# A gated mix of attention and a spectral filter on one core: input and inverse transform folded on GpSimd, one pool of exponential buffers, two chunks normalised by block transposes

## Chip, core and metric

The kernel runs on one core of one Trainium2 chip. The metric is the device time of one execution in microseconds (us); lower is better. A core has a matrix engine (TensorE, PE in the profile, with its weight loads listed apart as PEld), a vector engine (VectorE, DVE), an activation engine (ScalarE, ACT), a general-purpose engine (GpSimd, POOL) and an engine that only issues transfers here (SyncE, SP). SBUF is the working memory on the core, PSUM the accumulator memory to which TensorE writes.

## What is computed

Attention over 16 heads of 28 columns, and a two-dimensional real Fourier filter, both on the same x, mixed row by row by a sigmoid gate:

```python
def reference(A_x, A_wqkv, A_wo, B_x, B_w_r, B_w_i, gate_w):
    # x is [1, 2048, 448] bfloat16; H = 16 heads, Dh = 28
    def _A_ref(x, wqkv, wo):
        qkv = (x @ wqkv).reshape(B, S, 3, H, Dh).transpose(2, 0, 3, 1, 4)
        q, k, v = qkv[0], qkv[1], qkv[2]
        p = softmax(einsum("bhqd,bhkd->bhqk", q, k) * Dh ** -0.5)
        o = einsum("bhqk,bhkd->bhqd", p, v)
        return o.transpose(0, 2, 1, 3).reshape(B, S, D) @ wo
    def _B_ref(x, w_r, w_i):
        X = rfft2(x.astype(float32), axes=(-2, -1)) * (w_r + 1j * w_i)
        return irfft2(X, s=(S, D), axes=(-2, -1)).astype(bfloat16)
    x = A_x
    g = sigmoid((x * gate_w).sum(-1, keepdims=True))
    return g * _A_ref(x, A_wqkv, A_wo) + (1 - g) * _B_ref(x, B_w_r, B_w_i)
```

The filter takes A_x as its input too (B_x is not used). With 448 columns there are F = 225 frequencies along a row, and 2F = 450 real numbers per row after that transform.

## The kernel before

**Attention.** The heads form four groups of four (g), the 2048 queries four blocks of 512 (qc). A *chunk* is one group with one block: chunk c = 4g + qc, 16 chunks in order. A chunk has 64 *units*, one for each of 16 key tiles (kt) and four heads (j); a unit is a 128 x 512 tile of scores. TensorE makes the scores in PSUM (L1059). Most units get their exponential on ScalarE, two units to an instruction of 128 x 1024 (L1082, from the two `psA` tiles). The others, called D units here, are done on VectorE by an integer trick: `z` turns a 128 x 512 score tile in a `psX` bank into the bit pattern of a bfloat16 power (L1113), and two *shifts* add constants to it (L1137, on a pair of units, 128 x 1024 int16), so that three terms together approximate the exponential. The second shift is always on GpSimd, the first goes to VectorE or GpSimd. An A unit is one value product on TensorE (L1154), a D unit three. Value products accumulate in one bank, `psV`, for the chunk; one row of it holds the sum of the exponentials.

**Normalisation.** When a chunk's products are complete, `close` copies `psV` to `Oraw` (DVE), sends the sums through DRAM and back (`dS`, `Ssm`), inverts them and multiplies by the gate's odds (L1208, L1209, DVE), sends the result through DRAM into a broadcast tile `Rbc`, and multiplies on GpSimd into the block's `qT` tile (L1215), which is free by then. The last chunk instead goes through `finale`: 32 x 32 block transposes on DVE from `psV` and back (L1239 to L1248), in two halves, with no transfer.

**Filter.** Beside the attention run *fillers*: projections, and the transform in stages. `fa`: x times cosines and sines along the columns, four products over 112 rows each of the transposed x (`xT`) with 450 columns moving; `fae`: eviction to `bufB` (L689); `fb`: a 128-point transform over the rows with the constant `C1`, 450 columns; `fbe`: eviction (L694); `fx`: a transfer that rearranges `bufB` into `bufA`. Then per group of frequencies `fc`, the filter products `fm` (DVE, L718), `fy`/`fz` (GpSimd, L724, L726), `fd`, and `fde` (eviction to `VT`). `fp`: the inverse along the columns, four products of 448 moving columns for each of 16 tiles; `fpe`: eviction to `bufB` (L752). `output`: the last row transform (`C1T` times `bufB`) and the four groups' output projection accumulate in one bank, `oe` scales it into `fin` (L787 on DVE, L789 on ACT), `od` sends it out. Output tiles 4qc to 4qc+3 need the four normalised chunks of block qc, so tiles 8 to 11 wait for chunk 14, tiles 12 to 15 for chunk 15.

**Order.** Nothing is scheduled on the chip. While the program is built, a planner (`plan`, `dispatch`, `pick`) plays the five engines with assumed durations and writes each engine's instructions out in the order in which it started them; each engine then runs its list in that order and waits for its operands. `scores` issues a group of two A units and at most one D unit; `want_D` decides on the D unit from the VectorE and GpSimd work that the planner has outstanding, and needs a free pool entry. Exponentials of A units go to nine buffers `PA`, those of D units to four buffers `PZ` of three pairs each; at the start, until the values of the first group exist, the `PZ` buffers are lent to the A units (`early`), and no unit is a D unit in that time. Three `psX` banks serve all fillers and the D units.

## Time and profile before

| | |
|---|---|
| median of the runs | 408.09 us (410.72, 402.36, 408.09) |
| the profiled execution | 403.12 us, its span 401.3 us |
| mean granted TensorE clock in it | 0.995 |
| transfers | 18.40 MB on the queue that SP issues to, 22.6% of the 16 DMA engines' time |

The span runs from the first to the last instruction of the profiled execution; the time holds a little more than the span (1.8 us here). Busy times of an engine count overlapping instructions once. Groups of instructions are listed as line, engine, operation, what it writes and reads, shapes, count | busy time, mean duration of one | idle time of the engine ahead of them and what ended it.

### The profile page before, as it was taken

The page shows a single profiled execution, that of the slowest core. Times are in us where ns is not written, and L with a number is a line of the kernel's source. Part 1 is how long each engine was busy: PE and PEld are TensorE (multiplying, and loading weights), DVE is VectorE, ACT ScalarE, POOL GpSimd, SP SyncE. Part 2 cuts the span into 40 slices and gives each one's busy share as a digit, 9 for nine tenths or more (in the row PEclk, how much of TensorE's full clock was granted, in tenths as well). Part 3 has the DMA queues.
Part 4 walks back from the last instruction along what each step waited for, and adds up shares of the span by engine and source line. Part 5 has one row for each costly group of instructions (what it writes and reads, how often), then busy time and mean ns, then how long its engine had stood idle before and what let it go on. Part 6 is the DMA issues. An engine that isn't in the chain of part 4 may idle for free.

```text
span 401.3 us, 12448 instructions
## 1 busy us (share of the span) xinstructions
PE 378.2 (94%) x5140; PEld 127.5 (32%) x5140; DVE 328.2 (82%) x584; ACT 374.8 (93%) x415; POOL 239.0 (60%) x242
## 2 busy tenths in 40 slices
PE   6999999999998999998999999999999998999974
PEld 6553323323222222222333333333222222223232
DVE  0456697887999899998989999999989998888732
ACT  3999999999998999999999999999999999999932
POOL 4203355365566675745979899977739577654410
PEclk9999999999999999999999999999999999999989
DMA  7700014001974611114232211211010101010102
GB/s 212 184 5 2 4 6 69 3 4 32 93 98 67 69 27 35 32 26 99 82 67 56 65 47 42 73 26 42 4 28 3 29 5 29 15 59 20 54 9 93
DMA packets 41932, 19.19 MB, mean 48 GB/s; under 512 B 27884, under 2 KB 39524, under 8 KB 41876
## 3 DMA queue, kind: packets, MB, share of 16 engines
q1 hardware_dynamic: 41876, 18.40, 22.6%
q8 instruction: 40, 0.66, 0.7%
q14 instruction: 16, 0.13, 0.1%
HBM read 14.40 MB, written 2.09 MB: 41 GB/s over the span
## 4 chain that ended last, share of the span: by engine, by line
PE 41%; ACT 31%; DVE 13%; issue 8%; POOL 3%; DMA 2%; SPq 1%; DVEq 0%; ACTq 0%; POOLq 0%
ACT PA L1082 29%; PE psX L324 14%; PE psA L1059 13%; PE psV L1154 10%; DVE PZ L1113 6%; DVE PZ L1137 1%; POOL PZ L1137 1%; ACT PZ L1082 1%; PE psA L324 1%; DMA Wst<-in_B_w_r_dram 1%; PE psX L375 1%; DVE Rsm L1209 1%; PE psX L421 1%; DVE bufB L689 1%; DVE fin L787 1%
## 5 line engine op out<-in xcount | busy, mean ns | idle before, releaser
L1082 ACT ACTIVATE PA<-psA 128x1024 bf16<-128x1024 f32 x383 | 354.1, 1098 | 4.6 <-PE psX L1059 2.4
L1137 POOL TENSOR_SCALAR PZ<-PZ 128x1024 int16<-128x1024 int16 (+1 forms) x152 | 164.1, 1080 | 93.6 <-DVE PZ L1113 76.4
L1113 DVE TENSOR_SCALAR PZ<-psX 128x512 int16<-128x512 f32 x236 | 157.8, 682 | 21.8 <-PE psX L1059 19.2
L1059 PE MATMUL psA<-qT,kT 32*128 32x512 bf16 x788 | 152.5, 383 | 7.7 <-ACT PA L1082 7.1
L1154 PE MATMUL psV<-PZ,V 128*32 128x512 bf16 x730 | 117.9, 383 | 2.4 <-DVE PZ L1137 1.4
L1154 PE MATMUL psV<-PA,V 128*32 128x512 bf16 x766 | 115.5, 386 | 0.5 <-ACT PA L1082 0.5
L1059 PE MATMUL psX<-qT,kT 32*128 32x512 bf16 x236 | 90.5, 384 | 0.1
L1059 PEld LDWEIGHTS <-kT 32*128 32x128 bf16 x1024 | 42.3, 90 | 145.6 <-issue 143.5
L1137 DVE TENSOR_SCALAR PZ<-PZ 128x1024 int16<-128x1024 int16 (+1 forms) x90 | 54.8, 610 | 1.3
L1154 PEld LDWEIGHTS <-V 128*32 128x32 bf16 x1496 | 32.5, 94 | 48.8 <-issue 43.9
L324 PE MATMUL psX<-xT,Wp 112*32 112x512 bf16 x512 | 40.6, 384 | 0.9 <-ACT Wp L340 0.8
L1215 POOL TENSOR_TENSOR qT<-Oraw,Rbc 128x512 bf16<-128x512 f32 x15 | 19.5, 1300 | 6.7 <-DMA Rbc<-dR 5.9
L566 POOL TENSOR_TENSOR sqk<-qT 128x512 bf16<-128x512 bf16 x14 | 14.7, 1049 | 10.8 <-DVE qT L562 10.2
L718 DVE TENSOR_TENSOR T<-psX,Wst 128x450 bf16<-128x450 f32 x32 | 18.7, 614 | 1.7 <-PE psX L324 1.6
L324 PE MATMUL psX<-Bst,VT 113*32 113x448 bf16 (+1 forms) x256 | 20.1, 358 | 0.0
L324 PEld LDWEIGHTS <-xT 112*32 112x32 bf16 x768 | 14.6, 95 | 16.2 <-issue 13.6
L324 PE MATMUL psX<-Bst,xT 112*32 112x450 bf16 x256 | 18.9, 358 | 0.4 <-DVE PZ L1113 0.4
L324 PE MATMUL psX<-Wst,xT 112*32 112x336 bf16 (+1 forms) x448 | 18.2, 269 | 0.0
L516 POOL TENSOR_TENSOR sqk<-kT 128x512 bf16<-128x512 bf16 x12 | 12.7, 1055 | 4.8 <-DVE kT L505 3.1
L324 PEld LDWEIGHTS <-Wp 112*32 112x32 bf16 x512 | 10.1, 94 | 15.3 <-issue 13.5
L336 DVE COPY xT<-psX 112x1024 bf16<-112x1024 bf16 x4 | 2.8, 692 | 12.2 <-PE psX L421 12.2
L724 POOL TENSOR_TENSOR bufA<-T 128x225 bf16<-128x225 bf16 x16 | 9.0, 564 | 6.0 <-PE psX L1059 3.5
(90 smaller groups left out, 281.7 us busy)
## 6 DMA issues: line engine op xcount, KB each, us to landing
Rbc<-dR SPq DMA_DIRECT2D x15, 256.0 KB
IV<-c_IV SPq DMA_DIRECT2D x16, 128.0 KB
bufA<-bufB SPq DMA_DIRECT2D x16, 112.5 KB
bufA<-in_A_x_dram SPq DMA_DIRECT2D x4, 448.0 KB
out_dram<-fin SPq DMA_DIRECT2D x16, 112.0 KB
S<-c_S SPq DMA_DIRECT2D x16, 96.0 KB
Wst<-in_B_w_r_dram SPq DMA_DIRECT2D x7, 112.5 KB
Wst<-in_B_w_i_dram SPq DMA_DIRECT2D x7, 112.5 KB
```

What stands on the lines that cost most here:

```text
L324: self.nc.tensor.matmul(o[c:c + n], lhsT=w[:, c:c + n], rhs=r, start=start, stop=stop, tile_position=(0, c), skip_group_check=True)
L375: mms = [(128, lambda: nc.tensor.matmul(u.bank[:, 0:128], lhsT=self.ident, rhs=self.ident, start=True, stop=True)) for i in range(36)]
L516: e2 = self.ev(f"ks{g}{b}", {"POOL": 1120.0}, lambda e, b=b: nc.gpsimd.tensor_tensor(out=self.sqk[:, QW * b:QW * b + QW], in0=self.kT[g][: ...
L566: sq.append(self.ev(f"qs{g}{qc}", {"POOL": 1120.0}, lambda e, qc=qc: nc.gpsimd.tensor_tensor(out=self.sqk[:, QW * qc:QW * qc + QW], in0=se ...
L718: es.append(self.ev(f"fm{g}{ri}", {"DVE": t_dve(F2)}, lambda e, u=u, T=T, g=g, ri=ri: nc.vector.tensor_tensor(out=T[:, ri, :].rearrange("p ...
L724: y1 = self.ev(f"fy{g}", {"POOL": 520.0}, lambda e, T=T, g=g: nc.gpsimd.tensor_tensor(out=self.bufA[:, g, 0:F], in0=T[:, 0, 0:F], in1=T[:, ...
L1059: nc.tensor.matmul(out, lhsT=self.kT[g][32 * j:32 * j + 32, 128 * kt:128 * kt + 128], rhs=self.qT[g][qc][32 * j:32 * j + 32, :], start=Tru ...
L1082: e = self.op("exp", {"ACT": t_act(QW * n)}, lambda o: self.nc.scalar.activation(out=self.PAv[slot][:, 0:n, :], in_=self.PSA[i][:, 0:n, :] ...
L1113: e = self.op("z", {"DVE": t_dve(QW)}, lambda o: self.nc.vector.tensor_scalar(out=zt, in0=ub.bank, scalar1=float(ZBASE), scalar2=0.0, op0= ...
L1137: en.tensor_scalar(out=self.PZ[q][:, 1 + s, 0:n, :], in0=self.PZ[q][:, 0, 0:n, :], scalar1=1.0, scalar2=float(SHIFTS[s]), op0=ALU.mult, op ...
L1154: self.nc.tensor.matmul(self.PSV[32 * j:32 * j + 32, :], lhsT=self.V[:, kt, 4 * (i // NQ) + j, :], rhs=rhs, start=first, stop=False, tile_ ...
L1215: n = self.ev(f"n7_{c}", {"POOL": 1240.0}, lambda e: nc.gpsimd.tensor_tensor(out=self.qT[g][qc][:], in0=self.Oraw[r][:], in1=self.Rbc[r][: ...
```

## The change

1. **Folding of the input.** Columns d and D-d of x share their cosine and have opposite sines. GpSimd now forms sums and differences (`fo`, 128 x 4 x 223 bfloat16, eight instructions) and copies columns 0 and 224 (`fe`, four instructions) into `XF`, which occupies the memory of `VT`. The second input is read with a step of -1. `fa` is now the 128-point row transform (x as weights, `C1` moving, 4 times 128 columns); its eviction goes to a new tile `AT` (113 x 512); `fb` is the column transform, four products of 225 columns. `fx` waits for all folds, too.
2. **Folding of the inverse.** `fp` makes the even and the odd part apart (two products of 225 and two of 223 columns for each tile), and GpSimd forms their sum, their difference (written with a step of -1) and two edge columns into `bufA` (`fs`, `fd`, `fu`: three instructions for each of 16 tiles). `output` reads `bufA` there.
3. **One pool of 24 buffers** `P` for A and D units from the start; the `early` lending is gone. `scores` may issue two D units in a group, and D units near a chunk's end are allowed. The limit on outstanding GpSimd work is 5000 instead of 4000 planner ns and counts only work that is due.
4. **Chunk 14** is normalised in `turned` by block transposes on DVE instead of the path through DRAM. Its four output tiles are planned 3 us after its close instead of 12 us, and the first part of output tiles 12 to 15 (all but the last group's product) is planned ahead of the end, 14 us after chunk 14's close.
5. The constants change with it: `small` 256 to 288 KB, `Bd` and `Bv` halved; the gate's odds are loaded for the last two blocks (eight small transfers instead of four).

```diff
+        for tg in range(4):
+            ts = slice(4 * tg, 4 * tg + 4)
+            lo, hi = self.bufA[:, ts, 1:F - 1], self.bufA[:, ts, D - 1:F - 1:-1]
+            for k, op in enumerate((ALU.add, ALU.subtract)):
+                fs.append(self.ev(f"fo{tg}{k}", {"POOL": 1950.0}, ... nc.gpsimd.tensor_tensor(
+                    out=self.XF[:, ts, (F if k else 1):(D if k else F - 1)], in0=lo, in1=hi, op=op), [self.xp[tg]], pr, rel=pr - 8e3))
...
-            mms = [self.mm(F2, ..., lhsT=... self.xT[0:112, c, 128 * t:128 * t + 128], rhs=lambda c=c: self.Bd[:, c, :], ...) for c in range(4)]
+            for ch, d0 in enumerate((0, HF - 1, F, D - HF)):
+                mms.append(self.mm(128, ..., lhsT=lambda t=t, d0=d0: self.XF[:, t, d0:d0 + HF], rhs=lambda: self.C1, ...))
...
+            mms = [self.mm(F, ..., lhsT=lambda A=A, ch=ch: A[:, ch, :], rhs=lambda ch=ch: self.Bd[0:HF, ch, :], ...) for ch in range(4)]
...
-            b1.append(self.dma(f"fx{t}", ..., [e] + self.xall, pr + 4, slack=3000.0))
+            b1.append(self.dma(f"fx{t}", ..., [e] + self.xall + fall, pr + 4, slack=3000.0))
...
-                    mms.append(self.mm(D, ..., rhs=lambda fn=fn, ch=ch, ri=ri: self.Bv[0:fn, ch, ri, :], ...))
+                    mms.append(self.mm(c1 - c0, ..., rhs=lambda fn=fn, ch=ch, c0=c0, c1=c1: self.Bv[0:fn, ch, c0:c1], ...))
+                es = [self.ev(f"fs{t}", {"POOL": 520.0}, ... out=y[:, t, 1:F - 1], in0=even, in1=odd, op=ALU.add ...),
+                      self.ev(f"fd{t}", {"POOL": 520.0}, ... out=y[:, t, D - 1:F - 1:-1], in0=even, in1=odd, op=ALU.subtract ...),
+                      self.ev(f"fu{t}", {"POOL": 70.0}, ...)]
...
-        self.NPA = 9
-        self.NPZ = 4
+        self.NP = 24
...
-        if len(us) == 3 and self.want_D(t, us):
+        while len(ds) < 2 and len(us) >= 3 and self.want_D(t, us[:3 + len(ds)], len(ds)):
+            ds.append(None)
...
-        return self.dve_work(t) < 900.0 and self.pool_work(t) < 4000.0
+        return self.dve_work(t) < self.DT1 and self.pool_work(t) < self.POOLT
...
+    def turned(self, e, g, qc, r):
+        e = self.ev("u1", {"DVE": 600.0}, ... nc.vector.transpose(out=self.Rbc[r][:], in_=self.Oraw[r][:]), ...)
+        e = self.ev("u2", {"DVE": 160.0}, ... nc.vector.reciprocal(out=R, in_=self.Rbc[r][:, ONE:QW:32]), ...)
+        e = self.ev("u3", {"DVE": 80.0}, ... nc.vector.tensor_tensor(out=R, in0=R, in1=self.oddsT[:, 0, :], op=ALU.mult), ...)
+        e = self.ev("u4", {"DVE": 600.0}, ... nc.vector.tensor_tensor(out=blk(self.nq[0][:]), in0=blk(self.Rbc[r][:]), in1=R..., op=ALU.mult), ...)
+        e = self.ev("u5", {"DVE": 600.0}, ... nc.vector.transpose(out=self.qT[g][qc][:], in_=self.nq[0][:]), ...)
+        self.outputs(qc, self.norm_d[qc], self.now + 3e3)
+        for b in range(4):
+            self.output(4 * (NQ - 1) + b, None, self.now + 14e3 + 100 * b, True)
```

285 lines of the change are left out of this document (169 added, 116 removed).

## The prediction

> **What bounds the kernel now.** I read the page's busy shares first, then the groups by line, then windows cut where chunk 0 begins its exponentials and where chunks 1, 2, 3 and 15 do (found by counting exponentials along the program's order), then the end in the timeline.
>
> ```profile
> PE 378.2 (94%) x5140; PEld 127.5 (32%) x5140; DVE 328.2 (82%) x584; ACT 374.8 (93%) x415; POOL 239.0 (60%) x242
> L1082 ACT ACTIVATE PA<-psA 128x1024 bf16<-128x1024 f32 x383 | 354.1, 1098 | 4.6 <-PE psX L1059 2.4
> L1082 ACT ACTIVATE PZ<-psA 128x1024 bf16<-128x1024 f32 x11 | 10.9, 1102 | 0.4 <-PE psA L1059 0.4
> ...
> 13.70:45.00 31.30, 30.80 (x637) 13.19 (x635) 16.37 (x27) 30.82 (x38) 7.90 (x11) 1.00 0.13 31
> 45.00:69.00 24.00, 23.94 (x333) 7.46 (x333) 19.81 (x37) 24.00 (x29) 12.53 (x12) 1.00 0.22 29
> 69.00:93.10 24.10, 23.86 (x330) 7.37 (x326) 20.03 (x35) 23.98 (x27) 12.37 (x12) 1.00 0.10 16
> 93.10:361.50 268.40, 258.29 (x3340) 79.43 (x3328) 248.29 (x444) 263.98 (x289) 190.89 (x191) 1.00 0.24 46
> 361.50:384.70 23.20, 21.00 (x244) 6.53 (x241) 16.14 (x28) 23.20 (x26) 10.85 (x9) 0.98 0.13 35
> 384.70:401.30 16.60, 10.02 (x164) 5.10 (x161) 5.34 (x14) 2.32 (x5) 0.00 (x0) 0.91 0.17 56
> ```
>
> In a window's row stand its start and end, its length, then the busy time of PE, PEld, DVE, ACT and POOL (instructions in brackets). ScalarE is the bound: 394 exponentials stand idle for 4.6 + 0.4 us in all, and cost (354.1 + 10.9)/394 = 0.926 us each, since they overlap. In every window up to 384.7 it is busy for 98% or more. TensorE is nearly as full, but its matmuls overlap, and it waits for ScalarE as well. VectorE is the third: 16.37 of 31.30 in chunk 0, but 248.29 of 268.40 (92.5%) in chunks 3 to 14. So the kernel is a head of 13.7 us, a ScalarE stretch of 371.0 us and a tail of 16.6 us, in which ScalarE is nearly idle.
>
> **The change part by part.** *Exponentials moved.* In the changed program's order I count 384 exponentials (394 before) and 256 D units (236): 79, 281 and 24 exponentials in chunks 0 to 2, 3 to 14 and 15, against 83, 286 and 25; and 34, 207 and 15 D units against 27, 195 and 14. ScalarE's own saving is thus 4 x 0.926 = 3.7 us, 5 x 0.926 = 4.6 us and 0.9 us. In chunks 0 to 2 VectorE, at 56.21 of 79.40 us, has room for seven more units, so I take 3.7; only chunk 0, where TensorE too is busy for 30.80 of 31.30 us, could cut this: 1.9 is left if TensorE gives back only one of the three exponentials saved there.
>
> *VectorE in chunks 3 to 14.*
>
> ```profile
> L1113 DVE TENSOR_SCALAR PZ<-psX 128x512 int16<-128x512 f32 x236 | 157.8, 682 | 21.8 <-PE psX L1059 19.2 <-POOL PZ L1137 0.4 <-PE psV L1154 0.4
> L1137 DVE TENSOR_SCALAR PZ<-PZ 128x1024 int16<-128x1024 int16 x84 | 52.2, 623 | 1.2
> L1137 DVE TENSOR_SCALAR PZ<-PZ 128x512 int16<-128x512 int16 x6 | 2.6, 432 | 0.1
> L689 DVE CAST bufB<-psX 128x450 bf16<-128x450 f32 x16 | 9.9, 616 | 0.6 <-PE psX L324 0.6
> 260.00:285.00 25.00, 24.59 (x369) 8.24 (x370) 24.37 (x48) 25.00 (x28) 18.78 (x23) 1.00 0.14 33
> ```
>
> Twelve more `z` at 157.8/236 = 0.669 us are 8.0 us; six more full shifts at 52.2/84 = 0.621 are 3.7; three fewer half shifts at 0.43 give back 1.3; sixteen evictions to `AT` of 512 columns for 450 add 16 x 0.062 x 0.9 = 0.9. VectorE's load there rises from 248.3 to 259.6 us. Then the lock between VectorE and GpSimd:
>
> ```profile
> 365.81 1.05 POOL L1137 TENSOR_SCALAR PZ<-PZ 128x1024 int16<-128x1024 int16 x1
> 365.86 1.27 DVE L1137 TENSOR_SCALAR PZ<-PZ 128x1024 int16<-128x1024 int16 x1
> 367.76 0.43 DVE L1137 TENSOR_SCALAR PZ<-PZ 128x1024 int16<-128x1024 int16 x1
> 367.88 1.21 POOL L1137 TENSOR_SCALAR PZ<-PZ 128x1024 int16<-128x1024 int16 x1 [1.03 <-DVE PZ L1113]
> ```
>
> A VectorE shift takes 0.43 us where it starts first, and 1.27 where a GpSimd instruction has begun 0.05 us ahead: it waits for that one's end. So the mean of 623 ns holds 0.19 us of waiting a shift. GpSimd gets about a fifth more work (below), which raises this to some 0.22 a shift: 72 shifts, 2 us. The load becomes 261.6 us. The trace of before shows how full VectorE can be while ScalarE keeps its pace: 24.37 of 25.00 us, 97.5%, in the window from 260 to 285, with ScalarE busy throughout. At that share chunks 3 to 14 take 261.6/0.975 = 268.3 us, no gain; at ScalarE's saving they take 263.8, for which VectorE must be 99% full. I take the middle, 2.3 us gained, and keep 4.6 gained and 1.6 lost (270 us, a share of 97%) as ends.
>
> The Trainium skill, "SBUF — State Buffer", section "Who interferes with whom", says that this port pair is locked for a whole instruction and that "Issue order, not op shape, decides who blocks." The trace agrees: 1.27 against 0.43 us for the same shift. By that rule a fold holds VectorE's shifts up for its whole length, which would make my 2 us a lower end.
>
> *GpSimd.*
>
> ```profile
> L1137 POOL TENSOR_SCALAR PZ<-PZ 128x1024 int16<-128x1024 int16 x146 | 160.3, 1098 | 91.4 <-DVE PZ L1113 74.5 <-PE psX L1059 3.3 <-DVE Rsm L1208 2.6
> L566 POOL TENSOR_TENSOR sqk<-qT 128x512 bf16<-128x512 bf16 x14 | 14.7, 1049 | 10.8 <-DVE qT L562 10.2 <-PE psX L1059 0.3
> L726 POOL TENSOR_TENSOR bufA<-T 128x225 bf16<-128x225 bf16 x16 | 10.2, 639 | 0.3
> L1215 POOL TENSOR_TENSOR qT<-Oraw,Rbc 128x512 bf16<-128x512 f32 x15 | 19.5, 1300 | 6.7 <-DMA Rbc<-dR 5.9
> ```
>
> Fourteen more full shifts are 15.4 us, one half shift less gives back 0.6. A fold of 892 columns lies between 1.05 + 380 x (1.049 - 0.639)/287 = 1.6 and 892/512 x 1.049 = 1.8 us, eight of them 14 us; 32 sums of 223 columns at 0.64 are 20; twenty copies of two or eight columns, between nothing and the 0.64 of such a sum, lie under 13, and I take 3, as they are so much shorter; one normalisation less, 1.3. That makes 239 + 50 = 289 us of some 390, so GpSimd is not the bound. No row shows a step of -1: between nothing and doubling for the 24 instructions that have it, 0 to 24 us more (I take 0, as both neighbours in the rows are plain); even then it is 80% full, and the price would come through the lock. Folds stand behind shifts and squares of chunks 0 to 3, where GpSimd is busy 12.53 of 24.00 us; what queues behind one waits 1.8 us at most. `fx` waits for the folds on SP, but the folds lie in chunks 1 to 3 of the order, ahead of it.
>
> *TensorE.* `fa` and `fb` go from 2250 columns a tile to 1412, `fp` from 1792 to 896; forty more value products come to it.
>
> ```profile
> L324 PE MATMUL psX<-Bst,xT 112*32 112x450 bf16 x256 | 18.9, 358 | 0.4 <-DVE PZ L1113 0.4
> L324 PE MATMUL psX<-Bst,VT 113*32 113x448 bf16 x128 | 11.5, 358 | 0.0
> L324 PE MATMUL psX<-Bst,VT 112*32 112x448 bf16 x128 | 10.9, 358 | 0.0
> L1154 PE MATMUL psV<-PA,V 128*32 128x512 bf16 x766 | 115.5, 386 | 0.5 <-ACT PA L1082 0.5
> ```
>
> At 18.9/(64 x 450) and 22.4/(64 x 448) us a column these are 8.8 + 11.2 us less, the value products 40 x 0.151 = 6.0 more: 14 us less, all of it beside ScalarE and VectorE. I count nothing; it is what lets TensorE serve the extra D units without becoming late. Small transfers gain and lose little: four issues of chunk 14's path through DRAM go, four loads of odds come; `small` lands ahead of a head in which nothing waits for it.
>
> *The tail.*
>
> ```profile
> 383.84 1.48 PE psV L1154 x7
> 385.40 0.80 DVE L1239 STREAM_TRANSPOSE psX<-psV 128x256 f32<-128x256 f32 x2 [6.27 <-PE psV L1154]
> 387.26 0.76 DVE L1248 STREAM_TRANSPOSE qT<-nq 128x256 bf16<-128x256 bf16 x2
> 390.12 0.68 DVE L787 TENSOR_SCALAR fin<-psA,omg 128x448 bf16<-128x448 f32 x1 [2.10 <-issue]
> 390.85 1.15 PE psA L324 x20
> 392.03 0.68 DVE L787 TENSOR_SCALAR fin<-psA,omg 128x448 bf16<-128x448 f32 x1 [1.23 <-PE psA L324]
> 395.48 0.68 DVE L787 TENSOR_SCALAR fin<-psA,omg 128x448 bf16<-128x448 f32 x1 [0.85 <-PE psA L324]
> 397.96 0.63 ACT L789 ACTIVATE fin<-psA,omg 128x448 bf16<-128x448 f32 x1 [0.61 <-DMA out_dram<-fin]
> 383.04 1.27 POOL L1215 TENSOR_TENSOR qT<-Oraw,Rbc 128x512 bf16<-128x512 f32 x1 [3.00 <-DMA Rbc<-dR]
> ```
>
> The last value products end at 385.3, 16.0 us ahead of the end. The block transposes end at 388.0; then output tiles 8 to 11 pass one after the other through one bank, TensorE and VectorE in turn, 1.9 us each, because chunk 14's normalisation ended at 384.3 only; the last tile's scaling ends at 398.6, and its transfer 2.7 us later. In the new order tiles 8 and 9 are scaled before or inside the transposes, 10 and 11 have a bank each, and tiles 12 to 15 lack only their last product. Counted from the last value product: three tiles of 20 matmuls (1.15 us each by 390.85, about 0.9 without the bounce), four of 16 and four of 4 keep TensorE for about 6.5 us; VectorE's last two scalings end near 7.9; the transfer adds 2.7: 10.6 instead of 16.0. But one output tile (1 us) and six value products now stand between the last exponential and the last value product. I take 4.0 us gained; ends 5.0 and 2.0, the latter if VectorE is late. In chunk 15 VectorE gets `turned` (two transposes and a product of 512 columns, about 2.8 us by the halves' rows), one D unit and one scaling more: 16.14 becomes about 19.5 of 22.3 us, so the 0.9 us of its one exponential is taken, with 0 as the other end.
>
> **Sum.** 3.7 + 2.3 + 0.9 + 4.0 = 10.9 us off the profiled execution's 403.12 (span 401.3 and 1.8 around it): 392.2 us. That execution lies 1.2% under the median of the runs shown, 408.09, and near the fastest, 402.36; since a new median may lie as far above a quiet execution or not, I forecast 395 us. The ends of the terms are 3.7 + 4.6 + 0.9 + 5.0 = 14.2 and 1.9 - 1.6 + 0 + 2.0 = 2.3 us: 389 to 401.
>
> **Rivals.** *The whole saving, chance 0.12.* ScalarE stays the bound in chunks 3 to 14: 389 us. For it: 25.00 of 25.00 beside a VectorE at 97.5%. Against: that held for 25 us, not for 260.
> *VectorE takes over, 0.25.* Chunks 3 to 14 last as long as before, and the tail's gain shrinks with VectorE's lateness: 2.3 to 6 us off, 397 to 401 in a quiet execution, up to 406 by the spread of the runs. Speaks for it: 261.6 us of load for a stretch of 264 to 268.
> *GpSimd's lock makes it slower, 0.11.* As in the rows of 365.81 and 365.86, every fold, sum and shift on GpSimd that starts first holds a VectorE shift up. If the mean shift of VectorE grows from 0.62 to 0.82 us, 72 shifts add 14 us to 259.6; at 97.5% chunks 3 to 14 take 281 us, 12 more, and with late D units the tail gives nothing: 403.1 + 12.6 - 3.7 = 412, or 417 at the median's level. The kernel is slower at all from a mean of 0.70 on, by 2% from 0.81. Against it: the mean of 0.62 lies far nearer to 0.43 than to 1.27, and the folds lie where VectorE is not full.
>
> **How the numbers follow.** The forecast has 0.52, the rivals 0.12, 0.25 and 0.11. I count 2% (8 us), which is about what measurements of this kernel can tell from no change. Of the forecast's case 0.39 lies beyond 8 us off, with the first rival's 0.12 and a little of the second's 0.03: faster 0.54; the rest of these, 0.35, within 2%; slower 0.11. The range from 386 to 407 holds the first three cases but for their edges.
>
> **What would show it.** Right: 384 exponentials at 0.92 us or less; VectorE at 96% or more in chunks 3 to 14; ScalarE idle there for a few us more than before; output tiles 8 to 11 no longer 1.9 us apart at the end; last value product to end 11 us. Wrong: a mean VectorE shift over 0.70 us; folds of 3 us; ScalarE waiting for `psX` scores by tens of us; a first exponential later than 13.7 us.

## The result, and the profile after

The changed kernel takes 408.15 us (median of 20 runs) and the kernel before 402.94 us (20 runs beside them). The ratio is 1.0116 [1.0086, 1.0146]: slower by 1.2%, where 395 us had been forecast. Ratios leave out executions that took over 1.5% longer than the kernel's fastest, in which TensorE's clock was lowered for longer; medians hold them, so the two need not fit (*shifts to GpSimd* below has a median of 408.21 us and a ratio under 1).

The profiled execution of the changed kernel took 405.87 us, its span 404.0 (403.12 and 401.3 before). The page's busy shares and three groups by line, which answer to the first lines shown of before:

```profile
PE 369.2 (91%) x5372; PEld 132.1 (33%) x5372; DVE 348.5 (86%) x615; ACT 365.6 (91%) x402; POOL 287.3 (71%) x314
L1138 ACT ACTIVATE P<-psA 128x1024 bf16<-128x1024 f32 x384 | 357.4, 1082 | 18.9 <-PE psX L1115 12.3 <-PE psA L1115 6.3
L1180 DVE TENSOR_SCALAR P<-P 128x1024 int16<-128x1024 int16 (+1 forms) x95 | 61.0, 645 | 1.1
L699 POOL TENSOR_TENSOR VT<-bufA 128x892 bf16<-128x892 bf16 x8 | 14.2, 1778 | 0.1
```

ScalarE does the 384 exponentials, and its busy time falls by 9.2 us, as counted. But it now stands idle ahead of them for 18.9 us instead of 5.0, mostly until TensorE has made scores in `psX`, and its share falls from 93 to 91%. TensorE is less busy too. VectorE rises from 328.2 to 348.5 us and GpSimd from 239.0 to 287.3, both about as reckoned.

The windows, cut at the same exponentials of the program's order as before (chunks 0 to 2, chunk 4 alone, 3 to 14, 15, tail). The columns are start and end, length, busy time of PE, PEld, DVE, ACT, POOL, then the granted clock, the DMA engines' share and their GB/s:

```profile
13.60:90.80 77.20, 75.49 (x1272) 27.95 (x1276) 62.13 (x105) 75.16 (x88) 52.30 (x49) 1.00 0.16 23
114.00:142.60 28.60, 23.26 (x297) 6.85 (x292) 20.62 (x37) 21.74 (x24) 19.92 (x20) 0.85 0.61 75
90.80:367.90 277.10, 254.85 (x3584) 85.38 (x3572) 258.57 (x460) 261.22 (x284) 215.87 (x240) 0.98 0.24 43
367.90:391.30 23.40, 21.50 (x272) 6.61 (x268) 19.12 (x33) 22.45 (x25) 14.66 (x18) 1.00 0.10 32
391.30:404.00 12.70, 7.73 (x158) 4.49 (x150) 6.37 (x16) 1.28 (x3) 0.00 (x0) 0.99 0.26 83
```

| part | predicted | measured |
|---|---|---|
| chunks 0 to 2 | -3.7 | 79.4 to 77.2: -2.2 |
| chunks 3 to 14 | -2.3 (ends -4.6, +1.6) | 268.4 to 277.1: +8.7 |
| chunk 15 | -0.9 | 23.2 to 23.4: +0.2 |
| tail | -4.0 | 16.6 to 12.7: -3.9 |
| head | 0 | 13.7 to 13.6: -0.1 |
| sum | -10.9 | 401.3 to 404.0: +2.7 |

The tail is as worked out. Everything turns on chunks 3 to 14, 8.7 us longer where 2.3 less were forecast. One of them stands out: chunk 4 takes 28.6 us, and the granted clock there is 0.85. In the kernel before, its window and the two rows of chunk 3's sums read:

```profile
115.80:139.60 23.80, 22.13 (x272) 6.11 (x268) 21.80 (x36) 22.13 (x25) 15.78 (x16) 1.00 0.60 75
127.90 0.39 SPq L295 DMA_DIRECT2D Ssm<-dS  x1
131.20 0.23 DVE L1208 RECIPROCAL Rsm<-Ssm 128x16 f32<-128x16 f32 x1
```

The timeline of the changed kernel shows what happens in it there:

```profile
123.71 0.47 SPq L302 DMA_DIRECT2D Ssm<-dS  x1
124.23 3.56 SPq L302 DMA_DIRECT2D Wst<-in_B_w_i_dram  x4
133.93 0.25 DVE L1254 RECIPROCAL Rsm<-Ssm 128x16 f32<-128x16 f32 x1 [4.31 <-DMA Ssm<-dS]
135.52 0.58 PE L1115 MATMUL psX<-qT,kT 32*128 32x512 bf16 x1 [4.19 <-DVE P L1160]
138.15 1.02 ACT L1138 ACTIVATE P<-psA 128x1024 bf16<-128x1024 f32 x1 [5.46 <-PE psX L1115]
139.66 1.02 ACT L1138 ACTIVATE P<-psA 128x1024 bf16<-128x1024 f32 x1 [0.49 <-PE psA L1115]
```

In brackets stands the idle time ahead of an instruction and what ended it. The transfer of chunk 3's sums is issued at 123.71 among loads of the filter's weights on the same queue, and lands only when the reciprocal starts, 10.2 us later. The reciprocal's place in VectorE's order comes 4.31 us before that; VectorE runs in order, so the `z` steps behind it wait, their `psX` banks stay full, TensorE stands 4.19 us, ScalarE 5.46 us. From 134.16 on TensorE has half its clock for 10.24 us, and the exponentials come every 1.5 us (139.66 after 138.15) instead of every 0.9.

Two theories follow. **Theory 1, the stall:** the late sums and the half clock behind them make up the loss. **Theory 2, VectorE:** VectorE's load is what the chunks run into, so ScalarE's saving can't be had; the stall comes on top. A third, the lock between VectorE and GpSimd, had been a rival in the prediction.

### The profile page after: what moved, and what is told of

Read it like the earlier page. It is cut to its first block, busy times and chain, and to the rows that moved or that the text cites. A ratio compares the mean times of both kernels' runs of the same rounds, so it can differ in the third digit from the quotient of the medians.

```text
span 404.0 us, 13077 instructions
## 1 busy us (share of the span) xinstructions
PE 369.2 (91%) x5372; PEld 132.1 (33%) x5372; DVE 348.5 (86%) x615; ACT 365.6 (91%) x402; POOL 287.3 (71%) x314
## 4 chain that ended last, share of the span: by engine, by line
PE 52%; DVE 24%; ACT 10%; issue 6%; DMA 4%; POOL 3%; SPq 0%; DVEq 0%; ACTq 0%; POOLq 0%
PE psX L331 18%; PE psA L1115 18%; PE psV L1198 12%; DVE P L1160 10%; ACT P L1138 10%; DVE P L1180 6%; DMA Ssm<-dS 3%; POOL P L1180 1%; DVE bufB L779 1%; PE psX L383 1%; DVE T L746 1%; DVE Oraw L343 1%; PE psX L1115 1%; PE psX L429 1%; DMA out_dram<-fin 1%
## 5 line engine op out<-in xcount | busy, mean ns | idle before, releaser
L1138 ACT ACTIVATE P<-psA 128x1024 bf16<-128x1024 f32 x384 | 357.4, 1082 | 18.9 <-PE psX L1115 12.3
L1180 POOL TENSOR_SCALAR P<-P 128x1024 int16<-128x1024 int16 x165 | 176.3, 1069 | 61.9 <-DVE P L1160 44.8
L1160 DVE TENSOR_SCALAR P<-psX 128x512 int16<-128x512 f32 x256 | 170.5, 680 | 19.5 <-PE psX L1115 17.4
L1198 PE MATMUL psV<-P,V 128*32 128x512 bf16 x1536 | 135.2, 387 | 6.0 <-DVE P L1180 3.6
L1180 DVE TENSOR_SCALAR P<-P 128x1024 int16<-128x1024 int16 (+1 forms) x95 | 61.0, 645 | 1.1
L331 PEld LDWEIGHTS <-Wp 112*32 112x32 bf16 x512 | 10.1, 95 | 21.6 <-issue 19.5
L331 PE MATMUL psX<-Wo,qT 128*32 128x448 bf16 x192 | 15.1, 356 | 0.0
L699 POOL TENSOR_TENSOR VT<-bufA 128x892 bf16<-128x892 bf16 x8 | 14.2, 1778 | 0.1
L331 PEld LDWEIGHTS <-VT 128*32 128x32 bf16 (+3 forms) x512 | 10.3, 96 | 11.6 <-issue 9.5
L331 PE MATMUL psX<-IV,bufA 128*32 128x256 bf16 (+2 forms) x256 | 12.9, 276 | 1.3 <-DVE P L1160 0.9
L834 DVE TENSOR_SCALAR fin<-psX,omg 128x448 bf16<-128x448 f32 x12 | 8.1, 674 | 6.5 <-PE psX L331 6.1
```

What stands on the lines that cost most here:

```text
L331: self.nc.tensor.matmul(o[c:c + n], lhsT=w[:, c:c + n], rhs=r, start=start, stop=stop, tile_position=(0, c), skip_group_check=True)
L699: fs.append(self.ev(f"fo{tg}{k}", {"POOL": 1950.0}, lambda e, ts=ts, k=k, op=op, lo=lo, hi=hi: nc.gpsimd.tensor_tensor(out=self.XF[:, ts, ...
L1138: e = self.op("exp", {"ACT": t_act(QW * n)}, lambda o: self.nc.scalar.activation(out=self.P[slot][:, 0:n, :], in_=self.PSA[i][:, 0:n, :], ...
L1160: e = self.op("z", {"DVE": t_dve(QW)}, lambda o: self.nc.vector.tensor_scalar(out=zt.bitcast(I16), in0=ub.bank, scalar1=float(ZBASE), scal ...
L1180: en.tensor_scalar(out=self.P[q[1 + s]][:, 0:n, :].bitcast(I16), in0=self.P[q[0]][:, 0:n, :].bitcast(I16), scalar1=1.0, scalar2=float(SHIF ...
L1198: self.nc.tensor.matmul(self.PSV[32 * j:32 * j + 32, :], lhsT=self.V[:, kt, 4 * (i // NQ) + j, :], rhs=rhs, start=first, stop=False, tile_ ...
```

## The experiments

Ratios are to the kernel before, run on the same chip. Where no other kernel is named, the edit is made in the changed one. In the recorded expectations the first four runs say theory A for theory 1, B for theory 2 and C for the lock, and names such as e6_both_apart (*both edits together*), e7_both_z (*the narrower z without the stall*) and e10_true_prices (*true prices*) stand for the runs.

### The stall: loads and normalisation

**Loads apart.** In `build`, ahead of writing the orders out; only SP's order changes:

```diff
+            t0 = 13e3 + 3.6 * 21.6e3
+            for o in self.order:
+                if o.kind == "dma" and o.name.startswith("sp") and o.start > t0:
+                    o.start = t0 + 2.0 * (o.start - t0)
```

> The changed kernel; every engine's list is the same, except that SyncE issues the 16 loads of the filter's weights at twice their spacing, so that fewer of them lie in the DMA queues ahead of chunk 3's sums. Theory A (the time is lost in chunk 4: the transfer of the sums takes 10.2 us behind the weight loads, VectorE waits 4.3 us at the reciprocal, ScalarE 5.5 us, and TensorE then runs at half clock for 10.2 us): the wait at the reciprocal falls under 1 us, chunk 4 lasts 22 to 24 us instead of 28.6, no half clock before the tail, and the time falls by 5 to 8 us to 397 to 401. Theory B (VectorE is full in chunks 3 to 14, wherever the transfers land): no more than 2 us.

Measured: 404.93 us, ratio 1.0038 [1.0001, 1.0074]. VectorE's wait shrank, but did not vanish; the timeline of this kernel:

```profile
130.77 0.25 DVE L1258 RECIPROCAL Rsm<-Ssm 128x16 f32<-128x16 f32 x1 [1.07 <-DMA Ssm<-dS]
```

Chunk 4 fell to 25.0 us. Yet TensorE's pause of 1.21 us was followed by 13.65 us of half clock, and chunk 5 took 26.0. The time fell by 3.2 us, between the figures of the two theories. The loads are thus one cause of the late sums, but not all of it: issued at 122.48, the sums still took 8.3 us here. And a short pause can be enough for the half clock to follow.

**The kernel before with loads apart**, the same edit:

> The same spacing of the weight loads in the kernel before. Its chunk 4 lasts 23.8 us for 24 exponentials that need 22.2. Theory A: it gains 0 to 2 us only, as its wait there is 1.7 us and its clock stays full, so that the changed kernel with the same spacing comes out level or ahead of it by up to 3 us. Theory B: both gain alike, and the changed kernel stays 4 to 5 us behind.

Measured: 402.61 us, ratio 0.9991 [0.9956, 1.0026]. The kernel before had nothing to gain here: its sums of chunk 3 are issued later, at 127.90, and its reciprocal at 131.20 finds them (the rows above show no wait). It stays 2.3 us ahead of the changed kernel with the same edit.

**Normalisation late**, a second way to take the wait away, without touching the loads:

```diff
+            for o in self.order:
+                if o.name[:3] in ("n3_", "n4_", "n5_", "n6_", "n7_") and 2 <= int(o.name[3:]) < 12:
+                    o.start += 4000.0
```

> The changed kernel, in which the steps that follow the arrival of a chunk's sums (reciprocal, product with the odds, two transfers, the product on GpSimd) stand 4 us later in their engines' orders for chunks 2 to 11; nothing else moves. Theory 1 (the sums of chunk 3 arrive late behind the weight loads, VectorE's order stands still on the reciprocal, TensorE pauses and is then granted half its clock): the wait of 4.3 us at the reciprocal falls under 1 us, chunk 4 from 28.6 to 24 to 25.5 us, no half clock near 134 us, and the time falls by 4 to 6 us, to 402 to 404. Theory 2 (VectorE is full, the wait only shows it): chunk 4 shortens, but chunks 5 to 7 give it back; the time stays within 1.5 us of the changed kernel's.

Measured: 402.86 us, ratio 1.0029 [1.0000, 1.0058]. Two windows of it, chunk 4 and chunks 3 to 14:

```profile
113.80:135.40 21.60, 20.11 (x301) 6.64 (x296) 21.31 (x37) 21.30 (x24) 18.24 (x18) 1.00 0.63 86
90.50:364.20 273.70, 253.55 (x3584) 85.42 (x3576) 260.65 (x460) 261.66 (x284) 215.52 (x240) 0.99 0.23 44
```

Chunk 4 fell from 28.6 to 21.6 us at full clock. But chunks 3 to 14 together fell by 3.4 us only, to 273.7: chunk 5 now takes 24.7 and chunk 11 23.3 (23.7 and 21.9 with the stall), with VectorE busy for 23.9 and 23.0 of them. So the stall costs 0.9% in all, as theory 1 has it, and half of the 7 us taken out of chunk 4 comes back in chunks where VectorE is full. Theory 2 had that for chunks 5 to 7 alone, and all of it.

**Both edits together:**

> The changed kernel with the later steps of the normalisation (4 us, chunks 2 to 11) and the weight loads twice as far apart in SP's order. Theory 1: neither a wait at the reciprocal nor a half clock between 100 and 380 us; chunks 4 and 5 take 24 and 23 us; 399 to 402 us, and chunks 6 to 14 as in the changed kernel, 201.5 us. Theory 2: as theory 1 in chunks 4 and 5, but half clocks return elsewhere, after the short pauses of TensorE that a full VectorE makes; the time stays above 403.

Measured: 402.75 us, ratio 1.0039 [1.0015, 1.0063], the same as with the late normalisation alone.

```profile
91.90:364.90 273.00, 253.37 (x3584) 85.40 (x3576) 259.67 (x460) 261.68 (x284) 215.65 (x240) 0.99 0.22 44
```

Chunks 3 to 14 take 273.0 us, still 4.6 more than before, with no wait for sums left and one half clock of 3.41 us (at 346.97). VectorE is busy for 259.67 of them, 95.1%. What remains to be explained is the difference from here to 266, where the forecast put them.

### VectorE's load

**A narrower z.** From chunk 3 on, `z` covers 448 of 512 columns; the other 64 keep old values, so part of the output is not computed. Every engine's order stays. First beside the stall:

```diff
         zt = self.P[q[0]][:, k, :]
+        w = QW - 64 if u[0] >= 3 else QW
-            out=zt.bitcast(I16), in0=ub.bank, ...
+            out=zt.bitcast(I16)[:, 0:w], in0=ub.bank[:, 0:w], ...
```

> The changed kernel with all orders kept, but from chunk 3 on the first exponential step on VectorE covers 448 of the 512 columns of a unit (the other 64 keep old values): 222 instructions 0.067 us shorter, 14.9 us of VectorE. Theory A: chunk 4's stall and half clock stay, the time falls by less than 3 us. Theory B: chunks 3 and 5 to 14 come back to ScalarE's pace, 0.92 to 0.93 us an exponential, which is 4 to 6 us off; chunk 4's stall alone stays.

Measured: 402.64 us, ratio 0.9974 [0.9932, 1.0017]. Chunk 4 still took 28.2 us, but the time fell by 1.4% against the changed kernel.

**The narrower z without the stall**, on top of both edits:

> As e6_both_apart, and from chunk 3 on the z step of each D unit covers 448 of its 512 columns (64 columns of each such block of probabilities keep older values, so that part of the output is not computed), which takes about 0.06 us each, 13 us in all, off VectorE. Theory 1: no faster than e6_both_apart by more than 1 us, since ScalarE sets the pace once the stall is gone. Theory 2: 3 to 5 us below e6_both_apart, and chunks 8 to 13, in which VectorE is busy for 97% or more, shorten by 2 us or more together. Both true: 394 to 397 us, which is the saving of the exponentials as forecast.

Measured: 393.55 us, ratio 0.9788 [0.9723, 0.9853]. The whole stretch in one row:

```profile
90.80:357.40 266.60, 250.14 (x3584) 85.24 (x3576) 243.23 (x460) 260.29 (x284) 218.35 (x241) 0.99 0.22 45
```

Chunks 3 to 14 fall to 266.6 us, and VectorE's share of them to 91.2%; the prediction had put them at 266.1. This is 9.2 us less time than with both edits alone, more than had been expected of either theory. VectorE lost 16.4 us, more than the narrower `z` explain: its shifts also wait less for GpSimd (57.8 us for 95, 65.0 in *both edits*).

**The kernel before with the narrower z**, the control:

> The kernel before, with the z step of each D unit from chunk 3 on over 448 of its 512 columns (part of the output is not computed), its orders unchanged: about 12 us less of VectorE's time. It is the counterpart of the step from e6_both_apart to e7_both_z, which gave 9.2 us. If the change moved the limit from ScalarE to VectorE: the kernel before gains little by it, 0 to 3 us (398 to 401 beside 401). If VectorE limits both kernels alike: 7 to 10 us here too (391 to 394).

Measured: 400.83 us, ratio 0.9973 [0.9934, 1.0012].

```profile
92.80:358.70 265.90, 257.44 (x3339) 79.00 (x3328) 237.68 (x443) 263.73 (x288) 190.38 (x191) 1.00 0.24 46
```

The same edit is worth 2.5% where the change is in, and about 0.3%, within its interval nothing, where it is not. In the kernel before, ScalarE sets the pace: 263.73 of 265.90 us. In the changed one, with the stall away, VectorE does. That shows theory 2, and a bound for its size: at most some 9 of the 12 us by which *both edits* miss the forecast's ratio of 392.2/403.12 = 0.973. It is a bound because the narrower `z` takes 16.4 us off VectorE, more than the 259.67 - 248.29 = 11.4 us that the change put on it in chunks 3 to 14.

**Fewer D units.** Both edits, and lower bounds in `want_D`, hence a new plan:

```diff
-        self.LASTD, self.DT1, self.DT2, self.MINX2, self.POOLT = 3, 900.0, 1000.0, 2, 5000.0
+        self.LASTD, self.DT1, self.DT2, self.MINX2, self.POOLT = 3, 700.0, 800.0, 2, 5000.0
```

> As e6_both_apart, but the planner's bounds on VectorE's queued work are 700 and 800 ns in place of 900 and 1000: 240 D units and 392 exponentials (256 and 384 in the changed kernel, 236 and 394 in the one before), with a new plan. By ScalarE alone (theory 1) the eight exponentials more cost 7 us: 3 to 7 us above e6_both_apart. By VectorE alone (theory 2) the sixteen D units fewer free about 14 us of VectorE: at or below e6_both_apart, with fewer pauses of TensorE and less half clock.

Measured: 406.18 us, ratio 1.0101 [0.9988, 1.0214], unclear. Giving units back to ScalarE did not help. It lies 3.4 us above *both edits*, in the range that theory 1 gave for ScalarE's extra work; but the profiled execution also had three half clocks of 6.8 us (from 298.5, 349.7 and 373.6), so the run does not decide between the two.

**True prices.** Both edits, and the planner's price for a full shift on VectorE raised from 0.34 to 0.64 us, which is what the profile shows (645 ns):

```diff
-            so = self.op("shift", {"DVE": 70.0 + 0.265 * QW * n, "POOL": 110.0 + 1.05 * QW * n}
+            so = self.op("shift", {"DVE": 70.0 + 0.56 * QW * n, "POOL": 110.0 + 1.05 * QW * n}
```

> As e6_both_apart, but the planner is told that a full shift on VectorE lasts 0.64 us (0.34 in the changed kernel; 0.645 measured), and makes a new plan: 395 exponentials and 234 D units, so nearly those of the kernel before. If VectorE's order was packed too full because its shifts are priced too low: few waits of ScalarE (under 10 us in all), chunks 3 to 14 at 268 us or less, 395 to 399 us in spite of 11 exponentials more. If the plan's prices do not matter and only the sum of both engines' work does: 402 to 406, as in e9_fewer_d.

Measured: 402.08 us, ratio 1.0022 [0.9995, 1.0049]. The planner, told the true price, itself goes back to 395 exponentials and 234 D units. ScalarE's idle time falls to 7.4 us, as expected, but 395 to 399 us were not reached. A new pause is in the way, at 299:

```profile
297.63 3.62 POOL L1187 TENSOR_SCALAR P<-P 128x512 int16<-128x512 int16 x4
300.60 0.40 PE L1205 MATMUL psV<-P,V 128*32 128x512 bf16 x4 [1.50 <-POOL P L1187]
```

TensorE waits 1.50 us for a shift that comes late on GpSimd. In the windows of the same kernel, the stretch behind that pause:

```profile
300.90:311.20 10.30, 10.05 (x76) 2.09 (x72) 5.45 (x9) 6.95 (x7) 9.74 (x15) 0.50 0.06 13
```

The clock is 0.50 although TensorE is busy for 10.05 of 10.30 us, and ScalarE is busy for only 6.95: 3.4 us are lost there.

### GpSimd: the lock, or its queue

**The inverse's fold undone on TensorE**, four products for each output tile in place of GpSimd's 48 sums and copies; no other edit, but a new plan follows from it:

```diff
-        self.COMB = 0
+        self.COMB = 16
```

> The changed kernel with the inverse's sums and differences left to TensorE (four products of 223 to 225 columns for each output tile instead of one of 448, no GpSimd sums): 48 GpSimd instructions, some 20 us, fewer, TensorE 3 us more. Theories A and B: chunks 0 to 11 unchanged, the whole within 2 us. Theory C (GpSimd's sums hold VectorE's shifts up): chunks 12 to 14 get 3 us shorter, and the mean VectorE shift there falls from 0.66 towards 0.55 us.

Measured: 408.41 us, ratio 1.0112 [1.0066, 1.0159]: no difference to the changed kernel. But its one profiled execution shows two effects against each other. It took 417.95 us, with half the clock for 41 us between 134 and 189, but full clock from 230 on. Chunks 12 to 14 of the changed kernel, then the same chunks and the tail of this one:

```profile
302.00:367.90 65.90, 58.85 (x751) 19.29 (x741) 63.02 (x109) 62.03 (x69) 59.89 (x78) 1.00 0.08 20
313.70:377.20 63.50, 57.95 (x755) 19.89 (x753) 60.16 (x102) 62.08 (x68) 49.02 (x46) 1.00 0.08 19
399.50:416.20 16.70, 10.86 (x290) 7.48 (x278) 7.06 (x17) 1.16 (x2) 0.00 (x0) 1.00 0.22 71
```

Chunks 12 to 14 are 2.4 us shorter, nearly the 3 us of theory C, but not by its mechanism: the mean of a full shift on VectorE rises there, from 677 to 747 ns. VectorE does less, since the new plan gives it 20 of these shifts for 24 and GpSimd more. The tail loses 4.0 us (12.7 before this edit; the last version below, with the same edit, has 14.4), where TensorE has 10.86 us to do instead of 7.73. Nothing here shows that the sums cost time by holding VectorE's shifts up.

**Sums apart.** As *true prices*, and the sums twice as far apart in GpSimd's order:

```diff
+            sums = [o for o in self.order if o.eng == "POOL" and o.name[:2] in ("fs", "fd", "fu")]
+            s0 = min(o.start for o in sums)
+            for o in sums:
+                o.start = s0 + 2.0 * (o.start - s0)
```

> As e10_true_prices (395 exponentials, VectorE's shifts priced as measured, normalisation later, loads apart), and GpSimd's 48 sums and copies that undo the inverse's fold stand twice as far apart in GpSimd's order. In e10_true_prices TensorE stood 1.50 us at 299.1 for a GpSimd shift that was queued behind such sums, and half the clock followed for 10.2 us. If GpSimd's queue is that pause's cause: no pause over 1 us between 290 and 310, no half clock there, 396 to 399 us, so 0.5 to 1.5% below the kernel before. If not: the pause stays and the time too, 401 to 403.

Measured: 403.23 us, ratio 1.0031 [0.9995, 1.0067]. The pause at 299 went and another came, in the timeline of this kernel:

```profile
334.15 0.61 POOL L795 TENSOR_TENSOR bufA<-bufB 128x223 bf16<-128x223 bf16 x1
334.71 0.61 POOL L797 TENSOR_TENSOR bufA<-bufB 128x223 bf16<-128x223 bf16 x1
335.29 3.30 POOL L1191 TENSOR_SCALAR P<-P 128x1024 int16<-128x1024 int16 x3
336.39 0.40 PE L1209 MATMUL psV<-P,V 128*32 128x512 bf16 x4 [1.33 <-POOL P L1191]
```

Two sums stand ahead of the shift that TensorE waits for, and 13.65 us of half clock follow from 338.70. The 396 to 399 us were missed, but the rows show what such a pause consists of.

**True prices with the sums on TensorE:**

> As e10_true_prices, with the undoing of the inverse's fold on TensorE (four products in place of one for each output tile) in place of GpSimd's 48 sums and copies. In e12_sums_apart the pause (1.33 us) only moved to 335.1, again for a GpSimd shift behind two sums. If GpSimd's queue makes these pauses: none over 1 us between 280 and 380 us, no half clock there, 396 to 400 us. If a shift on GpSimd comes late without sums too: pauses and half clock stay, 401 to 404.

Measured: 402.58 us, ratio 1.0021 [0.9987, 1.0054]. Between 280 and 380 us there was neither a pause over 0.6 us nor a half clock, as expected of GpSimd's queue; but a half clock came elsewhere, and the time stayed (396 to 400 us had been expected). The windows of this kernel ahead of it and in it:

```profile
180.00:187.00 7.00, 5.34 (x67) 1.84 (x64) 6.62 (x12) 7.00 (x9) 3.14 (x3) 1.00 0.31 82
187.10:197.40 10.30, 9.68 (x80) 2.11 (x78) 7.37 (x12) 7.11 (x8) 7.70 (x8) 0.50 0.31 83
```

Here ScalarE and VectorE did not stand still (7.00 and 6.62 of 7.00 us): TensorE had only 5.34 us of work in 7.00 us, in gaps of 0.6 us or less. That the input's fold, which took work from it, is the reason is not shown.

### A pause made on purpose

**The kernel before with one early reciprocal**, chunk 8's, put behind the issue of its transfer in the orders:

```diff
+            at = {o.name: o.start for o in self.order}
+            for o in self.order:
+                if o.name == "n3_8":
+                    o.start = at["n2_8"] + 1.0
```

> The kernel before, in which the reciprocal of chunk 8's sums alone stands directly behind the issue of their transfer, ahead of eleven other instructions of VectorE, so that VectorE stands still until the transfer lands (4 to 6 us more wait). If TensorE's pause sets off the half clock, as it seems after the stall of the changed kernel's chunk 4: 3 to 15 us of half clock begin within 4 us of the pause, and chunks 8 and 9 are longer by the stall and 1 to 5 us more. If the half clock comes from something else: chunks 8 and 9 are longer by the stall alone (2 to 4 us), at full clock.

Measured: 402.40 us, ratio 0.9986 [0.9949, 1.0023]. No wait arose, since the sums had landed by 235.74, where the reciprocal now stood: it tells nothing on the clock. The next edit moves the transfer as well:

```diff
+                if o.name in ("n2_8", "n3_8", "n2_11", "n3_11"):
+                    o.start = at["n1" + o.name[2:]] + (1.0 if o.name[1] == "2" else 2.0)
```

> The kernel before; the second transfer of the sums of chunks 8 and 11 stands directly behind the first in SP's order, and their reciprocal directly behind the copy of the values in VectorE's order, so that VectorE has nothing to do for the two transfers' length, some 4 us, twice (in e13_before_recip the sums had landed, and nothing waited). If TensorE's pause sets off the half clock: 3 to 15 us of half clock begin within 5 us of each wait, 4 to 10 us more in all, 405 to 411. If it comes from something else: the two waits alone, 2 to 6 us, at full clock, 404 to 408.

Measured: 412.69 us, ratio 1.0265 [1.0181, 1.0350]. Four rows of its timeline and the windows of the two chunks concerned, which take 23.6 and 20.9 us in the kernel before:

```profile
236.21 0.25 DVE L1212 RECIPROCAL Rsm<-Ssm 128x16 f32<-128x16 f32 x1 [2.94 <-DMA Ssm<-dS]
237.52 0.37 PE L1063 MATMUL psX<-qT,kT 32*128 32x512 bf16 x1 [1.79 <-DVE T L722]
308.37 0.25 DVE L1212 RECIPROCAL Rsm<-Ssm 128x16 f32<-128x16 f32 x1 [2.94 <-DMA Ssm<-dS]
309.22 0.37 PE L1063 MATMUL psX<-qT,kT 32*128 32x512 bf16 x1 [2.38 <-DVE PZ L1117]
```

```profile
228.50:256.10 27.60, 24.94 (x337) 8.06 (x329) 22.47 (x45) 23.76 (x27) 21.84 (x25) 0.94 0.18 47
301.60:325.70 24.10, 21.03 (x269) 6.12 (x261) 20.37 (x35) 21.41 (x25) 15.83 (x15) 1.00 0.06 14
```

Two waits of 2.94 us on VectorE lengthen the chunks by 4.0 and 3.2 us: even in the kernel before, where VectorE is busy for 92.5%, such a wait comes through to ScalarE in full. The median lies above both ranges that had been expected. Behind the pause of 1.79 us the clock was halved for 3.4 us (from 239.8); behind the longer one, 2.38 us, it was not. So a pause can be followed by half the clock, and need not be.

### The tail alone

**The kernel before with the last part of the change only** (`turned`, the four output tiles begun early, the odds of two blocks):

```diff
+        if qc == NQ - 2 and g == NG - 1:
+            return self.turned(e, g, qc, r)
...
-            p = self.pe(f"ow{t}a", u, mms[0:4], deps[0:3] + first, pr, first=True)
+            p = self.pe(f"ow{t}a", u, mms[:-1], self.norm_d[qc] + first, pr, rel=pr, first=True)
```

> The kernel before with the last part of the change alone: chunk 14 normalised by block transposes, and the last four output tiles started ahead of the last value products. Neither folds nor another set of buffers nor other rules for D units. If the tail's gain stands by itself: the last exponential to the end falls from 16.6 to 12.5 to 13 us, and the time by 3 to 4 us, to 397 to 398 beside 401. If it was the changed order of value products at the end that shortened the tail: under 1 us.

Measured: 403.15 us, ratio 1.0045 [1.0016, 1.0073]. In windows, chunks 3 to 14, chunk 15 and the tail:

```profile
91.80:363.90 272.10, 260.03 (x3342) 79.43 (x3331) 252.51 (x447) 266.71 (x291) 183.21 (x185) 1.00 0.24 46
363.90:387.60 23.70, 22.84 (x294) 6.99 (x297) 17.06 (x29) 23.59 (x27) 10.70 (x9) 1.00 0.10 30
387.60:400.20 12.60, 5.67 (x104) 2.50 (x96) 4.77 (x13) 1.28 (x3) 0.00 (x0) 0.78 0.17 56
```

The tail shortens by 4.0 us here, too, but the 397 to 398 us expected were not reached. The old planner's new plan has 397 exponentials instead of 394, two of them more in chunks 3 to 14 and one in chunk 15, and these take 272.1 and 23.7 us instead of 268.4 and 23.2. The tail's gain is real, and the stretch ahead of it takes it back. Three exponentials at 0.926 us make 2.8 of these 4.2 us; the rest is not explained, nor why the plan differs from chunk 6 on, long before `turned`.

### Relief without leaving anything out

**Shifts to GpSimd.** Both edits, and GpSimd may take a first shift as soon as VectorE has 300 ns of work ahead:

```diff
-        self.TH = 900.0
+        self.TH = 300.0
```

> As e6_both_apart, but the planner lets GpSimd take a first shift already when VectorE has 300 ns of work ahead (900 in the changed kernel); a new plan with 390 exponentials and 244 D units, 70 shifts on VectorE (95) and 182 on GpSimd (165). Nothing is left out of the computation. VectorE loses 25 shifts of 0.645 us and 12 z of 0.68: 24 us, to about 326; GpSimd gains 17 shifts of 1.07: 18 us, to about 305. If VectorE's load is what the change ran into (as e7_both_z says): 394 to 398 us, 1 to 2% below the kernel before, in spite of six exponentials more than in the changed kernel. If late shifts on GpSimd hold TensorE up instead (the pauses of e10_true_prices and e12_sums_apart): 401 to 405.

Measured: 408.21 us in the median of 11 (398.72 to 414.09), ratio 0.9961 [0.9924, 0.9998]. In its timeline VectorE, TensorE and, a little later, ScalarE wait for one product of the filter on GpSimd (L761):

```profile
206.19 1.16 DVE L753 TENSOR_TENSOR T<-psX,Wst 128x450 bf16<-128x450 f32 x2 [1.20 <-POOL bufA L761]
206.21 0.51 PE L338 MATMUL psX<-IV,bufA 128*32 128x256 bf16 x12 [1.46 <-POOL bufA L761]
207.35 1.94 ACT L1145 ACTIVATE P<-psA 128x1024 bf16<-128x1024 f32 x2 [3.34 <-PE psA L1122]
```

So VectorE's relief is real (249.8 us in chunks 3 to 14), but GpSimd, at 299.5 us, is now late with what it does in between, and these chunks take 273.5 us, no less than with both edits: the gain is 0.4%. Less load on VectorE helps only where the work does not become late on GpSimd instead.

**The same with the limit at 0 and the inverse's fold undone on TensorE** (`TH = 0.0`, `COMB = 16`):

> As e16_shifts_to_pool with the limit at 0 ns and the inverse's fold undone on TensorE: 387 exponentials, 250 D units, 63 shifts on VectorE, 191 on GpSimd, none of GpSimd's 48 sums and copies. VectorE about 325 us, GpSimd about 295. If both VectorE's load and GpSimd's queue count: 392 to 397 us, below e16_shifts_to_pool. If TensorE's 48 products more, or its half clock, take it back: 400 to 404.

Measured: 398.15 us, ratio 0.9897 [0.9865, 0.9928]: of the versions that compute the whole output, the one that is clearly faster than both kernels, if just short of the 392 to 397 us expected. The ratio is that of three executions (397.81 to 398.15 us); two more took 406.67 and 407.99. Page, groups and windows (chunks 3 to 14; 15; tail):

```profile
PE 368.9 (93%) x5552; PEld 137.9 (35%) x5552; DVE 333.5 (84%) x577; ACT 367.6 (93%) x405; POOL 290.3 (73%) x292
L1145 ACT ACTIVATE P<-psA 128x1024 bf16<-128x1024 f32 x387 | 359.4, 1101 | 7.2 <-PE psX L1122 3.3 <-PE psA L1122 2.3 <-issue 0.6
L1187 DVE TENSOR_SCALAR P<-P 128x1024 int16<-128x1024 int16 (+1 forms) x63 | 46.3, 737 | 2.5 <-DVE P L1167 0.5
```

```profile
92.00:358.30 266.30, 250.80 (x3602) 87.95 (x3594) 246.63 (x434) 261.34 (x284) 216.27 (x218) 1.00 0.21 46
358.30:381.70 23.40, 22.75 (x337) 7.68 (x333) 17.63 (x29) 23.33 (x26) 12.78 (x12) 1.00 0.09 28
381.70:396.10 14.40, 9.24 (x242) 6.99 (x232) 6.42 (x16) 1.20 (x2) 0.00 (x0) 1.00 0.21 66
```

VectorE does 333.5 us instead of 348.5, its share of chunks 3 to 14 is 92.6%, and they take 266.3 us. ScalarE's idle time falls to 7.2 us. The products for the fold cost 1.7 us in the tail (14.4 instead of 12.7). With three exponentials more than the changed kernel it is 2.2% faster, and 1.4% faster than *both edits*, on which it builds: what had to be saved was VectorE's time, not ScalarE's.

## Why the prediction was wrong

**Exponentials and VectorE's load: right.** 384 exponentials at 357.4/384 = 0.931 us (a little above the 0.92 that had been given as the sign), VectorE at 348.5 us, in chunks 3 to 14 at 258.6 to 260.7 against 261.6 worked out.

**Chunks 3 to 14: the step that failed.** "At that share chunks 3 to 14 take 261.6/0.975 = 268.3 us, no gain [...] I take the middle, 2.3 us gained." The share of 97.5% was read from one window of 25 us. Over the whole stretch VectorE reached 95.1% and ScalarE already waited; with the load as forecast, 261.6/0.951 = 275 us. In the kernels that keep ScalarE's pace the share is lower still: 92.5% before, 91.2% with the narrower `z`, 92.6% in the last version. The term was thus not between -4.6 and +1.6 us, but about +4.6 (273.0 against 268.4). In direction this is the second rival, "VectorE takes over", which gave 397 to 401 us for a quiet execution and up to 406, at a chance of 0.25; without the stall the kernel measures 402.8. But it, too, had these chunks no longer than before.

**The transfers: a term that was missing.** "Small transfers gain and lose little" held for those that come and go, but not for one that stays. Chunk 3's sums are issued at 123.71 instead of 127.90 and fall among the weight loads, and possibly other transfers (with the loads apart they still took 8.3 us); the reciprocal's place in VectorE's order no longer suits their landing. The stall and the half clock that came with it cost 4.1 us of the profile (277.1 against 273.0) and 0.8 to 0.9% of the time. No row of before showed the wait, but the prediction looked at GpSimd's and SP's queues only for what the change adds.

**Chunks 0 to 2 and 15.** The gain of 3.7 us was 2.2, within its bound of 1.9; chunk 15 gave nothing (+0.2), its other end. Both are small. The 2.8 us that the forecast added to 392.2, since a median might lie above a quiet execution, were not borne out either: the 20 runs of the kernel before have a median of 402.94 us, and the three shown ahead lay high.

**The tail: right,** -3.9 against -4.0, and -4.0 alone in the old plan. **GpSimd: right,** 287.3 us against 289, a fold 1.78 us against 1.6 to 1.8. The step of -1 shows no price: on GpSimd the changed kernel's sums of 223 columns take 0.657 us written forwards (L784), the differences 0.620 written backwards (L786), and the folds, which read one input backwards, 1.99 ns a column against 2.05 of the plain squares.

**The lock: right as a small term.** The mean shift is 0.645 us, against 0.65 reckoned and 0.70 from which the kernel would have been slower by it; in *both edits* it is 65.0/95 = 0.684. In the last version GpSimd takes 191 shifts instead of 165 and VectorE's mean shift is 0.737 us, but its 63 shifts still cost 15 us less than the 95 did. By the Trainium skill, "SBUF — State Buffer", section "Who interferes with whom", whichever of the two engines issues first holds the shared ports for its whole instruction. The prediction's rows agree with that (0.43 and 1.27 us); that the mean follows the number of GpSimd's shifts is not shown, since *both edits* has as many as the changed kernel. In two versions GpSimd held TensorE up in another way than the rival had it, through value products that wait for a shift behind sums in its queue (1.50 and 1.33 us); with the sums gone from there (402.58 us for 402.08) the time was the same.

What stays open: how much of the 0.8 to 0.9% is the half clock and how much the wait itself, since no run separates them; and what exactly decides whether a pause is followed by half the clock.

## What to carry to other kernels

A share that an engine holds for one good window is not what it holds over a long stretch: before work is moved to an engine that is above 92% busy, divide its new load by the share of the whole stretch. Here that would have been 261.6/0.925 = 283 us: too long by 10 us, but with the right sign. When two engines are both nearly full, count which of them the moved work loads per unit saved on the other, and look for a third with room. And an in-order engine that waits for a transfer pays in full when the transfer's queue becomes crowded, so after any new plan check where each reply lands against the place of the instruction that waits for it.
